# Gated linear attention and a feed-forward layer on one core: the decays of the first two chunk pairs written for both token parities on TensorE, one carried state added by matrix products, and a new written-out order

## The chip, the cores and the metric

The kernel runs on one core of one Trainium2 chip. The time is the device time of one launch in microseconds. Before the change its median over three runs is 182.09 us (181.44 to 182.46).

## The reference

There are two stages. The first is a gated linear recurrence over 768 tokens, for 4 batches of 8 heads with 48 elements each; the second is a feed-forward layer on the 3072 rows of 384 elements that come out of it.

```python
f = 1.0 / (1.0 + np.exp(-f_logit))                 # q, k, v, f_logit: (4, 8, 768, 48) float32
for t in range(S):
    state = f[:, :, t, :, None] * state + np.einsum('bhd,bhe->bhde', k[:, :, t], v[:, :, t])
    y[:, :, t] = np.einsum('bhd,bhde->bhe', q[:, :, t], state)
x = y.transpose(0, 2, 1, 3).reshape(3072, 384)
h = x @ w_in                                       # (384, 2048)
out = (h * np.cos(h)) @ w_out                      # (2048, 384)
```

## The kernel before

**Tiling.** The tokens are cut into 12 pairs of chunks. A pair is 256 tokens of one batch, three pairs to a batch, so pairs 0, 1, 2 are batch 0. Partition p holds the tokens 2p and 2p+1 of the pair, which the code calls the parities e = 0 and e = 1; g = 0, 1 are the two chunks of 128 tokens (the two halves of the partitions), u = 0, 1 are heads 0 to 3 and 4 to 7.

**Steps.** `describe` makes a graph of named steps; a step is one or a few instructions on one engine. For pair n:

- `f`, `k`, `q`, `v`: the loads (line 296), 384 KB each; for pairs 0 and 1 (`HALVES`) the loads of f, k and q are cut into two of 192 KB, `.0` and `.1`.
- `ex`, `ln` (ACT): log(1 + exp(-f)). `cum` (PE): its running sum over tokens, a product with a triangular matrix `incl`. `ei`, `eb` (ACT): exponentials of plus and minus that sum, the decays for k and for q; `eb` also holds the decay of a whole chunk.
- `fx`, `qa`, `ka` and, beyond pair 1, `ad`, `fy`: the running sum is kept for pairs of tokens alone, so the first token of each pair is corrected by hand: `ka` multiplies k by the gate that `fx` makes, `qa` multiplies q by 1 + exp(-f).
- `qm`, `km`: q and k times their decays, into the bfloat16 tile `qk`. `tq`, `tk`: the turn of `qk`, by TensorE with `qkt` as the copy out for pairs 0 to 3; for pairs 4 to 11 `tq` is one DMA transpose on SP's queue.
- `vb`, `vt`: v in bfloat16, and four rearranged copies of it.
- `sc` (PE), `am` (DVE): scores and their mask. `y`, `yi` (PE): the part from within the chunk and the part from the carried state. `xe`: the result as the feed-forward input x.
- `ps` (PE): products of k and v for the state. `st` (DVE): adds the carried state, in two halves of the partitions. `sz` (DVE): times the chunk's decay, giving the next state.

For the feed-forward unit m (the 256 tokens of pair m): `h` is the first product, eight steps of six matmuls; `co` (ACT) the cosine, `g` (DVE) the gate, four each; `o` the second product in row blocks 2m and 2m+1, four steps of four matmuls each; `ot` the copy out of PSUM, `out` the store. `w0.i` and `w1.i` load a quarter of w_in and w_out (768 KB) into a slot of `g`, `wc0.i` and `wc1.i` cast it to bfloat16. `zf` are matmuls on zeros; `ZEROS` is their number. `zsz`, `zqk`, `zsp`, `zvt` clear edges of buffers.

**Order.** `ORDER` lists every step with its engine (T PE, S ACT, V DVE, G POOL, Y SP's queue) and its buffer slots. Each engine runs its steps strictly in that order. Nothing reorders them at run time; an engine waits for what the step at its head needs.

```python
zf48:T2 zf49:T2 zf50:T2 zf51:T2 h0.11:T2 h0.10:T yi1:T7,6 st1.11:V sz1.11:V3 y1:T xe1.1:V2
```

Of the kernel before, what the change touches and what calls it, by code (L numbers as in the profile page):

```python
# [37 lines left out]
zf0:T0 zf1:T0 zf2:T0 zf3:T0 zf4:T0 zf5:T0 zf6:T0 zf7:T0 zf8:T0 zf9:T0 zf10:T0 cum0.0:T4 zvt.1:G
fx0.0:S zqk.0:G zsz.2:G k0.1:Y2 ka0.1:G cum0.1:T7 ei0.1:S1 km0.1:G0 eb0.0:S1 ei0.0:S ex1.0:S eb0.1:S
q0.0:Y0 v0:Y0 vb0:S0 ln1.0:S2 qa0.0:V qm0.0:V zsz.3:G zf11:T0 zf12:T0 zf13:T0 zf14:T0 zf15:T0  # L40
zf16:T0 zf17:T0 zf18:T0 zf19:T0 zf20:T0 zf21:T0 zf22:T0 zf23:T0 zf24:T0 cum1.0:T1 k0.0:Y ka0.0:G
km0.0:V zf25:T0 ps0.0:T6,7 f1.1:Y ex1.1:S ps0.1:T q0.1:Y ei1.0:S0 eb1.0:S0 ln1.1:S fx1.1:S qa0.1:V
sz0.01:V2 sz0.00:V st0.11:V f2:Y1 vt0.1:G2 zvt.0:V st0.10:V vt0.3:G qm0.1:G tk0.0:T0 tq0.0:T
qkt0.0:V0 v1:Y2 vt0.0:G ex2:S ln2:S1 k1.0:Y1 fx1.0:S zsp.1:G k1.1:Y zf26:T2 tk0.1:T6 zf27:T2 tq0.1:T
cum1.1:T3 qkt0.1:V1 zsz.1:G zsz.0:G zf28:T2 sc0.0:T4 am0.0:V2 sc0.1:T0 ad2:G0 sz0.10:V0 am0.1:V0
ei1.1:S eb1.1:S vb1:S1 vt1.2:S0 zf29:T2 zf30:T2 zf31:T2 zf32:T2 cum2:T2 ei2:S2 eb2:S2 ka1.0:V
zqk.1:G km1.0:V1 zf33:T6 zf34:T6 zf35:T6 zf36:T6 zf37:T6 zf38:T6 zf39:T6 zf40:T6 tk1.0:T4 ps1.0:T6,1
f3:Y0 ex3:S q1.0:Y1 sz0.11:V qa1.0:V q1.1:Y qa1.1:V qm1.1:V ln3:S0 fx3:S ka1.1:G vt0.2:G km1.1:G
ps1.1:T y0:T3,5 yi0:T xe0.0:S0 vt1.3:S vt1.1:S fy3:S st1.01:V st1.00:V sz1.01:V1 zf41:T0 zf42:T0
zf43:T0 tq1.1:T0 sz1.00:V qm1.0:G tq1.0:T qkt1.0:S2 tk1.1:T qkt1.1:V0 zf44:T2 zf45:T2 zf46:T2  # L50
zf47:T2 sc1.1:T6 xe0.1:V fx2:S ad3:G1 cum3:T0 ei3:S1 sc1.0:T4 am1.1:V1 am1.0:V3 w0.1:Y0 vt1.0:G
wc0.1:G zf48:T2 zf49:T2 zf50:T2 zf51:T2 h0.11:T2 h0.10:T yi1:T7,6 st1.11:V sz1.11:V3 y1:T xe1.1:V2
st1.10:V sz1.10:V eb3:S1 co0.1:S3 xe1.0:S g0.1:V3 fy2:S w0.0:Y1 wc0.0:G h0.01:T4 h0.00:T h1.01:T6
co0.0:S0 g0.0:V h1.00:T co1.0:S1 g1.0:V2 h1.10:T0 h1.11:T co1.1:S2 g1.1:V k3:Y2 ka3:G km3.1:G2
w0.3:Y4 wc0.3:G h0.31:T2 h0.30:T w0.2:Y0 wc0.2:G h1.21:T4 h1.20:T h0.20:T6 co0.3:S3 g0.3:V co1.2:S0
# [662 lines left out]
```

## Time and profile before

| what | us |
|---|---|
| median of three runs | 182.09 |
| span of the profiled execution | 179.3 |
| PE busy (share of the span) | 171.0 (95%) |
| DVE, ACT, POOL busy | 137.8, 131.3, 109.2 |
| zero matmuls (line 264), busy | 14.8 |
| first product (line 579), busy | 66.7 |
| second product (line 595), busy | 68.4 |

The span runs from the first to the last instruction of the profiled execution. That execution's own time is not listed apart; the three timed runs are 2.1 to 3.2 us longer than this span, so what lies around the span is taken as 182.09 - 179.3 = 2.8 us. A busy PE includes the zero matmuls, and a matmul counts as busy until its modelled end, so the busy share says when PE had something in hand, not that it ran at its peak.

### The profile page before, as it was taken

Reading aid. Unit: us, or ns where it says so; the run is one execution under the profiler, and the core shown is the slowest. Engines: PE = TensorE matmul, PEld = TensorE weight load, DVE = VectorE, ACT = ScalarE, POOL = GpSimd, SP = SyncE. Lnnn points to the kernel's source line nnn. Section 1 sums busy time; section 2 is a strip of 40 time slices with the busy share of each in tenths; the row PEclk is TensorE's granted clock in tenths of the full one; section 3 lists DMA queues with packets and bytes.
Section 4 is the critical chain, followed back from the end, with each engine's and each line's share of the span. In section 5 each row is a group of like instructions: output and inputs, shape, how many; then the busy total and the mean of one; then the engine's idle time right before and its main releaser. Section 6 shows DMA issues by size and latency. Waiting matters only on the chain.

```text
span 179.3 us, 5727 instructions
## 1 busy us (share of the span) xinstructions
PE 171.0 (95%) x2412; PEld 122.9 (69%) x2414; DVE 137.8 (77%) x206; ACT 131.3 (73%) x185; POOL 109.2 (61%) x139
## 2 busy tenths in 40 slices
PE   7998899999999999999999998999999999999992
PEld 2453568876578866778668885668877766867761
DVE  6379998998894989969899887768689996385330
ACT  3899878886999998988999979858973702364410
POOL 7498699976979998789977295827992000000000
PEclk9999999999999999999999999999999999999999
DMA  6999999999999799999999999959045900004013
GB/s 156 262 261 287 356 324 315 306 274 328 257 257 236 168 190 180 282 277 198 249 203 262 226 254 207 234 131 268 4 106 121 148 0 4 4 0 176 0 50 129
DMA packets 74394, 34.46 MB, mean 192 GB/s; under 512 B 67456, under 2 KB 72832, under 8 KB 74368
## 3 DMA queue, kind: packets, MB, share of 16 engines
q1 hardware_dynamic: 73696, 33.79, 81.4%
q8 instruction: 19, 0.31, 0.8%
q10 hardware_dynamic: 672, 0.30, 0.6%
q14 instruction: 7, 0.06, 0.1%
HBM read 25.17 MB, written 4.72 MB: 167 GB/s over the span
## 4 chain that ended last, share of the span: by engine, by line
PE 69%; DMA 10%; POOL 7%; SPq 5%; DVE 5%; issue 3%; ACT 0%; POOLq 0%; DVEq 0%; ACTq 0%
PE ps L595 29%; PE ps L579 29%; DMA q<-in_q_dram 7%; SPq L296 5%; PE ps L531 4%; DMA qkt<-qk 3%; PE ps L456 3%; POOL qk L404 3%; PE ps L479 1%; POOL sp L363 1%; PE ps L435 1%; DVE qk L404 1%; POOL vt L197 1%; DVE sz L503 1%; PE ps L374 1%
## 5 line engine op out<-in xcount | busy, mean ns | idle before, releaser
L561 DVE TENSOR_TENSOR g<-ps,co 128x1024 bf16<-128x1024 f32 x48 | 57.7, 1221 | 15.3 <-ACT co L584 11.3
L595 PE MATMUL ps<-w_out_bf,g 128*128 128x384 bf16 x384 | 68.4, 326 | 0.0
L579 PE MATMUL ps<-x,w_in_bf 128*128 128x256 bf16 x576 | 66.7, 273 | 0.4 <-issue 0.4
L584 ACT ACTIVATE co<-ps,halfpi 128x1024 bf16<-128x1024 f32 x48 | 52.6, 1115 | 17.7 <-PE ps L579 14.4
L579 PEld LDWEIGHTS <-w_in_bf 128*128 128x128 bf16 x576 | 55.8, 98 | 9.2 <-issue 0.6
L595 PEld LDWEIGHTS <-g 128*128 128x128 bf16 x384 | 36.0, 98 | 21.5
L461 DVE TENSOR_TENSOR am<-ps,pmask 128x1024 bf16<-128x1024 f32 x24 | 28.7, 1215 | 3.6 <-PE ps L456 3.5
L404 POOL TENSOR_TENSOR qk<-q,b 128x384 bf16<-128x384 f32 x22 | 21.9, 1002 | 2.6 <-DVE q L338 1.7
L404 POOL TENSOR_TENSOR qk<-k,bi 128x384 bf16<-128x384 f32 x22 | 21.9, 1007 | 1.6 <-ACT bi L391 1.1
L197 POOL COPY vt<-vb 64x384 bf16<-64x384 bf16 x31 | 15.9, 514 | 1.4
L264 PE MATMUL ps<-zero 128*128 128x512 bf16 x50 | 14.8, 435 | 1.3 <-DVE zero L203 1.2
L503 DVE TENSOR_TENSOR sz<-ps,b 64x192 bf16<-64x192 f32 x40 | 14.2, 354 | 1.9 <-PE ps L479 0.9
L351 POOL TENSOR_TENSOR k<-k,f 128x384 f32<-128x384 f32 (+1 forms) x13 | 11.7, 904 | 6.2 <-DMA k<-in_k_dram 2.9
L197 DVE COPY ot<-ps 128x384 f32<-128x384 f32 (+1 forms) x17 | 8.7, 519 | 8.5 <-PE ps L595 6.0
L341 POOL TENSOR_TENSOR q<-f,q 128x384 f32<-128x384 f32 x10 | 10.0, 999 | 8.1 <-DMA q<-in_q_dram 8.1
L363 POOL TENSOR_TENSOR sp<-ls 128x384 bf16<-128x384 f32 x10 | 10.3, 1029 | 4.4 <-issue 2.2
L497 DVE TENSOR_TENSOR ps<-ps,sz 64x192 f32<-64x192 f32 x32 | 11.7, 366 | 1.4 <-PE ps L479 0.3
L329 ACT ACTIVATE f<-f 128x768 f32<-128x768 f32 (+1 forms) x14 | 10.4, 748 | 2.7 <-DMA f<-in_f_logit_dram 2.5
L197 ACT CAST x<-ps 128x384 bf16<-128x384 f32 x12 | 5.5, 479 | 8.6 <-PE ps L531 8.6
L197 ACT COPY ot<-ps 128x384 f32<-128x384 f32 (+1 forms) x9 | 4.1, 455 | 8.9 <-PE ps L595 8.9
L456 PE MATMUL ps<-qkt 48*64 48x128 bf16 (+1 forms) x320 | 8.6, 219 | 1.9 <-DVE qkt L197 1.0
L264 PEld LDWEIGHTS <-zero 128*128 128x128 bf16 x52 | 5.1, 108 | 6.9 <-issue 2.5
(61 smaller groups left out, 166.2 us busy)
## 6 DMA issues: line engine op xcount, KB each, us to landing
v<-in_v_dram SPq DMA_DIRECT2D x12, 384.0 KB, 6.1
out_dram<-ot SPq DMA_DIRECT2D x22, 192.0 KB, 2.8
f<-in_f_logit_dram SPq DMA_DIRECT2D x10, 384.0 KB, 5.6
k<-in_k_dram SPq DMA_DIRECT2D x10, 384.0 KB, 6.1
q<-in_q_dram SPq DMA_DIRECT2D x10, 384.0 KB, 6.4
g<-in_moe_w_in_dram SPq DMA_DIRECT2D x4, 768.0 KB, 7.5
g<-in_moe_w_out_dram SPq DMA_DIRECT2D x4, 768.0 KB, 7.2
k<-in_k_dram SPq DMA_DIRECT2D x4, 192.0 KB, 5.0
```

The costliest lines, as they stand in the source:

```text
L197: (nc.scalar.copy if e == "ACT" else eng(e).tensor_copy)(out=o, in_=i)
L264: G.step(f"zf{i}", ("PE",), lambda e, dump=dump: nc.tensor.matmul(dump.ap, lhsT=zero[:, 0:128], rhs=zero, start=True, stop=True), writes=[ ...
L351: eng(e).tensor_mul(out=w.ap[:, :, 0, :], in0=w.ap[:, :, 0, :], in1=t.ap[:, :, 0, :])
L363: G.step(f"ad{n}", ("POOL",), lambda e: eng(e).tensor_add(out=sp.ap[:, 0, :, 0:D], in0=soft.ap[:, :, 0, :], in1=soft.ap[:, :, 1, :]), read ...
L404: G.step(f"{nm}{n}.{u}", ("POOL", "DVE") if cut else ("POOL",), lambda e, u=u, j=j, src=src, dec=dec: eng(e).tensor_mul(out=qkp[u][j].ap[: ...
L456: nc.tensor.matmul(o[t0:t1, r, 2 * a + g, :].rearrange("p (e n) -> p e n", e=2), lhsT=wide[s, t0 // 64, :] if turned else wide[s].rearrang ...
L461: G.step(f"am{n}.{u}", ("DVE",), lambda e, u=u, sc=sc: nc.vector.tensor_mul(out=am[u].ap.rearrange("p r b n -> p (r b) n"), in0=sc.ap.rear ...
L503: eng(e).tensor_mul(out=new.ap[s, :, r, :].rearrange("p (u a) n -> p u a n", u=2), in0=view()[s].rearrange("p (u a) n -> p u a n", u=2), i ...
L561: nc.vector.tensor_mul(out=o.rearrange("p b (n e) -> p b n e", e=2), in0=ph.ap.rearrange("p (b e n) -> p b n e", e=2, n=64), in1=co.ap.rea ...
L579: nc.tensor.matmul(ph.ap[:, i * T:(i + 1) * T].rearrange("p (g t) -> p g t", t=C), lhsT=w_in_bf[:, kk, f0:f0 + 128], rhs=xa[:, :, kk, :], ...
L584: G.step(f"co{m}.{j}", ("ACT",), lambda e, ph=ph, co=co: nc.scalar.activation(out=co.ap, in_=ph.ap, func=AF.Sin, bias=halfpi), reads=[ph], ...
L595: nc.tensor.matmul(po.ap[:, 0:DM], lhsT=gT.ap[:, j, i * C:(i + 1) * C], rhs=w_out_bf[:, j, :], start=(po.first and j == 4 * s), stop=(po.f ...
```

## The change

1. **Both parities on TensorE (pairs 0 and 1).** `cum` makes the running sum for each token and no longer for pairs of tokens: per half four products with `incl` or `strict` where there were two. `ei` and `eb` are twice as wide (384 and 388 columns instead of 192 and 196). `fx`, `qa` and `ka` of pairs 0 and 1 (four each) are gone; `qm` and `km` read a decay for each parity.
2. **Carried state by identity products (pair 1).** The four `st1` steps on DVE become `si1.0` and `si1.1` on PE, two products with the identity each, into the same PSUM bank as `ps1`.
3. **Loads.** On SP's queue f3, k3, q3 and v3 stand behind the w_in quarters. The first load is pair 1's f, and f0.0 goes from ACT's queue to SP's.
4. **`ZEROS`** 52 becomes 25, and `ORDER` is another for all 12 pairs and units.

The paths for `VLIE` are new but not taken, since `VLIE` is empty.

```diff
+VLIE = ()
+CARRY_PE = (1,)
-ZEROS = 52
+ZEROS = 25
 ORDER = """
-zvt.2:V zsp.2:V f0.1:Y0 zqk.2:G zsp.0:G f0.0:S ex0.1:S ln0.1:S2 f1.0:Y2 ex0.0:S fx0.1:S ln0.0:S
+f1.0:Y0 zf0:T2 f0.0:Y2 zf1:T1 f0.1:Y zsz.0:G zf2:T4 zsp.2:G v0:Y2 zsz.2:G k1.0:Y0 k0.1:Y1 f1.1:Y
...
+    bbS = slots("bb", [128, 2, 2 * HB + 4], F32)
+    bjS = slots("bj", [128, 2, 2 * HB], F32)
...
-        sp, bt, bi = Val(spS), Val(bS), Val(biS)
+        sp, bt, bi = Val(spS), Val(bbS if cut else bS), Val(bjS if cut else biS)
...
-            te, to = (t, t) if cut else (t.part(lambda a: a[:, :, 0, :]), t.part(lambda a: a[:, :, 1, :]))
+            if cut:
+                continue
+            te, to = t.part(lambda a: a[:, :, 0, :]), t.part(lambda a: a[:, :, 1, :])
...
+        W = HB * len(xe)
 
         def cum(e, o, h0, hn):
             w, un = sp.ap[:, :, h0:h0 + hn, :], hn // 4
-            o = o.ap[:, 0:un * (HB + 4)].rearrange("p (u c) -> p u c", u=un)
-            for x in xe:
-                nc.tensor.matmul(o[:, :, 0:HB], lhsT=incl,
-                                 rhs=w[:, x, :, 0:D].rearrange("p (u h) d -> p u h d", u=un),
-                                 start=(x == 0), stop=False)
+            o = o.ap[:, 0:un * (W + 4)].rearrange("p (u c) -> p u c", u=un)
+            for z in xe:
+                for x in xe:
+                    nc.tensor.matmul(o[:, :, HB * z:HB * z + HB], lhsT=strict if x > z and cut else incl,
+                                     rhs=w[:, x, :, 0:D].rearrange("p (u h) d -> p u h d", u=un),
+                                     start=(z == 0 and x == 0), stop=False)
...
-        for nm, dst, dh, sc, w in (("eb", bt, bth, -1.0, HB + 4), ("ei", bi, bih, 1.0, HB)):
+        for nm, dst, dh, sc, w in (("eb", bt, bth, -1.0, W + 4), ("ei", bi, bih, 1.0, W)):
...
+        both = [Val(ap=ident) for u in us] if n in CARRY_PE else []
         for u in us:
             G.step(f"ps{n}.{u}", ("PE",), lambda e, u=u: outer(e, u), reads=[qkp[u][1], vb],
-                   writes=[ps[g] for g in gs], sums=True)
+                   writes=[ps[g] for g in gs] + both[u:u + 1], sums=True)
...
-            if S0 is not None:
+            if S0 is not None and n in CARRY_PE:
+                def add(e, g=g, S0=S0):
+                    for r in range(2):
+                        nc.tensor.matmul(ps[g].ap[:, 0:HB].rearrange("p (a n) -> p a n", n=D), lhsT=ident,
+                                         rhs=S0.ap[:, :, r, :], start=(ps[g].first and r == 0),
+                                         stop=(ps[g].final and r == 1))
+                G.step(f"si{n}.{g}", ("PE",), add, reads=[S0] + both, writes=[ps[g]], sums=True)
+            elif S0 is not None:
```

Three places of the new order follow, each as it stood and as it stands. Row names give the buffer written, then those read.

On SP's queue before, from f3 on: f3, q1 (two halves), w_in's quarters 1 and 0, k3, w_in's 3 and 2, q3, then w_out's quarters 2 and 0.

```order
L296 DMA f_94<-in_f_logit_dram 128x8x96
L296 DMA q_101<-in_q_dram 128x4x96 x2
L282 DMA g_143<-in_moe_w_in_dram 128x3x512
L282 DMA g_144<-in_moe_w_in_dram 128x3x512
L296 DMA k_99<-in_k_dram 128x8x96
L282 DMA g_147<-in_moe_w_in_dram 128x3x512
L282 DMA g_143<-in_moe_w_in_dram 128x3x512
L296 DMA q_102<-in_q_dram 128x8x96
L282 DMA g_144<-in_moe_w_out_dram 128x4x384
L282 DMA g_147<-in_moe_w_out_dram 128x4x384
```

The two other quarters of w_out came four rows later, behind q2, k2 and v3. On SP's queue after, from k2 on (w_in's quarters 1 and 3 stand just ahead of it): k2, w_in's 0 and 2, q2, w_out's 1, 0 and 3, then f3, v2 and the last quarter, w1.2.

```order
L308 DMA k_100<-in_k_dram 128x8x96
L294 DMA g_149<-in_moe_w_in_dram 128x3x512
L294 DMA g_150<-in_moe_w_in_dram 128x3x512
L308 DMA q_101<-in_q_dram 128x8x96
L294 DMA g_152<-in_moe_w_out_dram 128x4x384
L294 DMA g_151<-in_moe_w_out_dram 128x4x384
L294 DMA g_148<-in_moe_w_out_dram 128x4x384
L308 DMA f_97<-in_f_logit_dram 128x8x96
L308 DMA v_106<-in_v_dram 128x8x96
L294 DMA g_152<-in_moe_w_out_dram 128x4x384
```

Pair 3's loads and the last weights have changed places; w1.2 goes into slot 4 of `g` (g_152), which wc1.1 must have read first.

POOL around the last weight cast, before: the k steps of pair 2 (qk_118), the last cast, then v of pair 2 (vb, vt), and the first steps of pairs 4 and 5.

```order
L404 TENSOR_TENSOR qk_118<-k_97,bi_116 128x8x48 x2
L197 COPY vt_125<-vb_121 64x8x48
L197 CAST w_out_bf<-g_144 128x1536
L197 CAST vb_122<-v_105 128x768
L197 COPY vt_124<-vb_122 64x8x48 x4
L363 TENSOR_TENSOR sp_106<-ls_109 128x8x48
L363 TENSOR_TENSOR sp_108<-ls_110 128x8x48
L341 TENSOR_TENSOR q_102<-f_96,q_102 128x8x48
```

POOL around the last weight cast (the second of these two), after:

```order
L415 TENSOR_TENSOR qk_118<-k_100,bi_116 128x8x48
L195 CAST w_out_bf<-g_148 128x1536
L372 TENSOR_TENSOR sp_109<-ls_110 128x8x48
L195 CAST w_out_bf<-g_152 128x1536
L195 COPY vt_130<-vb_121 64x8x48 x2
L359 TENSOR_TENSOR k_99<-k_99,f_97 128x8x48
L372 TENSOR_TENSOR sp_109<-ls_110 128x8x48
L415 TENSOR_TENSOR qk_120<-k_99,bi_115 128x8x48
L349 TENSOR_TENSOR q_101<-f_97,q_101 128x8x48
L415 TENSOR_TENSOR qk_120<-k_99,bi_115 128x8x48
L349 TENSOR_TENSOR q_102<-f_95,q_102 128x8x48
```

All of pair 3's work on POOL but its `ad` (the sp row between the casts) now follows the last weight cast, and pairs 4 and 5 follow that.

DVE before, from the second state of pair 0 (sz_135) to the first x: a mask of pair 0 (am_131), k and q of pair 1 with their corrections, `st` and `sz` of pair 1's first chunk (sz_136), and the copy qkt.

```order
L503 TENSOR_TENSOR sz_135<-ps_161,b_112 64x4x48
L461 TENSOR_TENSOR am_131<-ps_158,pmask 128x1024
L351 TENSOR_TENSOR k_98<-k_98,f_96 128x4x48
L404 TENSOR_TENSOR qk_118<-k_98,bi_114 128x8x48
L503 TENSOR_TENSOR sz_135<-ps_161,b_112 64x4x48
L338 SCALAR_TENSOR_TENSOR q_101<-f_96,q_101 128x4x48 x2
L404 TENSOR_TENSOR qk_118<-q_101,b_111 128x8x48
L497 TENSOR_TENSOR ps_161<-ps_161,sz_135 64x192 x2
L503 TENSOR_TENSOR sz_136<-ps_161,b_111 64x4x48 x2
L197 COPY qkt_126<-ps_158 128x1024
L197 CAST x_139<-ps_160 128x384
```

DVE after, the same stretch:

```order
L240 MEMSET qk_118 128x32x8
L537 TENSOR_TENSOR ps_166<-ps_166,sz_140 64x192
L543 TENSOR_TENSOR sz_142<-ps_166,bb_124 64x4x48
L415 TENSOR_TENSOR qk_119<-q_102,bb_125 128x8x48
L493 TENSOR_TENSOR am_136<-ps_165,pmask 128x1024
L195 COPY qkt_135<-ps_164 128x1024
L493 TENSOR_TENSOR am_137<-ps_166,pmask 128x1024
L493 TENSOR_TENSOR am_139<-ps_164,pmask 128x1024
L543 TENSOR_TENSOR sz_140<-ps_165,bb_125 64x4x48 x2
L493 TENSOR_TENSOR am_138<-ps_164,pmask 128x1024
L543 TENSOR_TENSOR sz_143<-ps_163,bb_125 64x4x48 x2
L195 CAST x_145<-ps_163 128x384
```

The corrections of q and k (L338, L351) and pair 1's additions are gone from it; three masks now stand ahead of pair 1's first state (sz_140 from ps_165), and a clearing of qk_118 has moved here from POOL.

More of the change, by code (lines that the diff above doesn't have):

```diff
@@ L38 @@
[L38 to L55, printed above, removed]
```

223 lines of the change are left out of this document (138 added, 85 removed).

## The prediction

> **What bounds the kernel now.** I read the page first, then the chain of waits, then stretches. The page's lines give the span and the busy engines.
>
> ```profile
> span 179.3 us, 5727 instructions
> PE 171.0 (95%) x2412; PEld 122.9 (69%) x2414; DVE 137.8 (77%) x206; ACT 131.3 (73%) x185; POOL 109.2 (61%) x139
> ```
>
> The chain (start, duration, what) shows three parts.
>
> ```profile
> 15.37 0.34 DVE sz L503
> ...
> 25.08 1.31 PE ps L579 x12
> ...
> 43.85 0.65 PE ps L595 x4
> ...
> 168.21 7.81 PE ps L595 x48
> ...
> 176.05 0.33 ACT ot L197
> ...
> 176.40 0.36 DVE ot L197
> ```
>
> Until 25.08 DVE and the loads lead to the first feed-forward product; from there to 176.02 PE is the chain but for a detour that costs it little; 3.28 us of copying and storing close it. The stretches (length, then busy PE, PEld, DVE, ACT, POOL, then clock, DMA share, GB/s) say how full PE is.
>
> ```profile
> 25.08:44.50 19.42, 19.42 (x264) 15.45 (x262) 17.28 (x22) 15.72 (x17) 16.31 (x16) 1.00 1.05 309
> 72.10:176.02 103.92, 102.89 (x1432) 76.05 (x1432) 78.18 (x105) 70.08 (x93) 48.97 (x58) 1.00 0.69 149
> 5.00:15.00 10.00, 8.86 (x110) 5.26 (x110) 6.18 (x12) 8.85 (x23) 7.49 (x13) 1.00 1.27 262
> 19.00:23.00 4.00, 3.43 (x95) 2.11 (x95) 3.78 (x9) 3.37 (x7) 3.63 (x4) 1.00 1.11 342
> ```
>
> PE has no idle time from 25.08 to 44.50 and 1.03 us after 72.10. So the end can move only by an earlier first product, by new waits after it, or by the tail. PE's real work after the first product is nearly the same: by steps, the new order puts cum3 (about 0.3 us) and si1.1 (0.2) behind it and yi1 (0.4) ahead, +0.1 us. The fillers on zeros (14.8 us busy) all stand ahead of it and cost only what the wait there leaves.
>
> **Loads.** Consumers that waited give landings: the first half load of f, q0.1 (the tenth half) and w1.3.
>
> ```profile
> 4.04 0.52 ACT L329 ACTIVATE f<-f 128x384 f32<-128x384 f32 x1 [1.50 <-DMA f<-in_f_logit_dram]
> 10.56 0.38 DVE L338 SCALAR_TENSOR_TENSOR q<-f,q 128x192 f32<-128x192 f32 x1 [0.20 <-DMA q<-in_q_dram]
> 44.65 1.46 POOL L197 CAST w_out_bf<-g 128x1536 bf16<-128x1536 f32 x1 [1.30 <-DMA g<-in_moe_w_out_dram]
> ```
>
> At 262 GB/s a half load (197 KB) takes 0.75 us, at 342 GB/s a weight quarter (786 KB) 2.3. From 4.0 on that puts the tenth half at 10.75 (10.56 measured) and w1.3, behind 28 more halves and 8 quarters, at 43.4 (44.65). The new queue then lands k0.0 at 11.5, k1.1 at 16.0, q1.1 at 16.8, w1.0 at 33.6 and w1.2, behind 25 halves and 8 quarters, at 41.2; by the 1.2 us that the check missed, 42.4. I take 41.8.
>
> **Parts and their prices** (line, engine, form, count, then busy us and mean ns):
>
> ```profile
> L347 ACT ACTIVATE f<-sp 128x192 f32<-128x192 bf16 x4 | 1.4, 354 | 0.1
> L338 DVE SCALAR_TENSOR_TENSOR q<-f,q 128x192 f32<-128x192 f32 x4 | 1.4, 363 | 2.6 <-DMA q<-in_q_dram 2.6
> L351 POOL TENSOR_TENSOR k<-k,f 128x192 f32<-128x192 f32 x3 | 1.8, 591 | 2.2 <-DMA k<-in_k_dram 2.1
> L391 ACT ACTIVATE bi<-ps 128x192 f32<-128x192 f32 x4 | 1.3, 328 | 0.9 <-PE ps L380 0.9
> L395 ACT ACTIVATE bi<-ps 128x384 f32<-128x384 f32 x10 | 4.7, 489 | 1.5 <-PE ps L380 1.5
> L497 DVE TENSOR_TENSOR ps<-ps,sz 64x192 f32<-64x192 f32 x32 | 11.7, 366 | 1.4 <-PE ps L479 0.3
> L503 DVE TENSOR_TENSOR sz<-ps,b 64x192 bf16<-64x192 f32 x40 | 14.2, 354 | 1.9 <-PE ps L479 0.9
> L461 DVE TENSOR_TENSOR am<-ps,pmask 128x1024 bf16<-128x1024 f32 x24 | 28.7, 1215 | 3.6 <-PE ps L456 3.5
> L404 DVE TENSOR_TENSOR qk<-q,b 128x384 bf16<-128x384 f32 x2 | 2.5, 1234 | 0.7 <-ACT b L391 0.6
> L404 DVE TENSOR_TENSOR qk<-k,bi 128x384 bf16<-128x384 f32 x2 | 1.1, 558 | 0.7 <-POOL k L351 0.7
> L197 DVE COPY qkt<-ps 128x1024 bf16<-128x1024 bf16 x6 | 4.0, 677 | 0.1
> L561 DVE TENSOR_TENSOR g<-ps,co 128x1024 bf16<-128x1024 f32 x48 | 57.7, 1221 | 15.3 <-ACT co L584 11.3
> L584 ACT ACTIVATE co<-ps,halfpi 128x1024 bf16<-128x1024 f32 x48 | 52.6, 1115 | 17.7 <-PE ps L579 14.4
> L584 ACT ACT_TABLE_LOAD x5 | 6.4, 1283 | 0.1
> ```
>
> Both parities: ACT loses four fx (1.4 us) and pays eight wider exponentials, 8 x 0.16 = 1.3, nothing on balance. DVE loses four qa (1.4) and one ka, POOL three ka (1.8); the eight extra cum products are a few tenths of PE in a stretch full of fillers. Identity products: four st of 0.366 leave DVE. All this counts only as far as it lies on the way to the first product, which I now follow.
>
> ACT's two exponentials of pair 1 begin at 4.0, those of pair 0 when f0.1 has landed (5.5); four steps of 0.52, then ei1.0, ei0.1, eb1.0, eb0.1, ex1.1, eb0.0 and ei0.0 at 0.5 end at 11.1. km0.0 on POOL starts with k0.0 at 11.5 and ends at 12.5; PE, with fillers and cum1.1 queued ahead, has ps0.0 at 13.4. From here DVE is the chain: four sz, two st and a clearing, 2.5 us, to 16.0; qm1.0; am0.1, qkt1.0, am0.0, am1.0 and two sz, 5.0; some 0.3 of starts. yi1 (0.4) and a filler (0.2) follow on PE. qm1.0 costs 0.56 or 1.23, and these rows tell why:
>
> ```profile
> 7.74 0.99 POOL L404 TENSOR_TENSOR qk<-k,bi 128x384 bf16<-128x384 f32 x1 [1.13 <-ACT bi L391]
> 7.85 1.30 DVE L404 TENSOR_TENSOR qk<-q,b 128x384 bf16<-128x384 f32 x1 [0.57 <-ACT b L391]
> 9.81 0.56 DVE L404 TENSOR_TENSOR qk<-k,bi 128x384 bf16<-128x384 f32 x1 [0.66 <-POOL k L351]
> ```
>
> Beside a running POOL product the same form ends 0.42 after POOL's end; alone it takes 0.56. km1.1 starts on POOL with k1.1 at 16.0, just when DVE comes to qm1.0. So the first product starts at 22.4 (0.56) to 23.1 (1.23); I take 22.8, 2.3 us before the 25.08 of now. The Trainium skill's page "SBUF — State Buffer", section "SBUF: two separate sides", states it as an exclusive lock: a DVE operation with two SBUF inputs and a GpSimd operation that reads SBUF exclude each other for a whole instruction. The rows agree; by that rule with POOL first the product starts at 23.1, without any lock at 22.4, which reaches the end only in the first rival below.
>
> **What takes the head start back.** The first co begins some 3.0 us after the first product (an h step 0.65, y1 0.6 behind am1.1, si1.1 and a filler 0.4, an h step 0.65, and what shows of the 1.28 us reload of ACT's table, 0.7). Seven co at 1.115, fy2 (0.5) and wc1.0 (1.46 like the cast above), with 0.4 of waits for g, bring ACT to 22.8 + 13.2 = 36.0, when o3.0 may start; the h steps, held to DVE's 1.22 a gate, are done before that. Nine o steps and pair 2's small products, 6.8 us, then lead PE to o1.2 at 42.8. o1.2 needs w1.2: landed 41.8, cast by POOL 1.46, 43.3. w1.2 must also wait for its slot; wc1.1 frees it near 33, and 7 us for the transfer fit in. So o1.2 starts at 43.2 and the early start has become a wait of some tenths at the last weight.
>
> How does that stand to now? At 44.50 in the chain (the end of the row at 43.85) the old order has 130.7 us of PE steps left by my count at the chain's prices (0.65 an h or o step; 1.3 us of idle come on top); at o1.2 the new one has 131.25. 44.50 + 130.7 = 175.2 against 43.2 + 131.25 = 174.45: 0.75 us gained here.
>
> **POOL and the transposes.** Behind wc1.2 POOL has all of pair 3 and then 4 and 5: 20 products, 8 vt, 2 vb until km5.0.
>
> ```profile
> 57.72 2.92 POOL L404 TENSOR_TENSOR qk<-k,bi 128x384 bf16<-128x384 f32 x3
> L197 POOL COPY vt<-vb 64x384 bf16<-64x384 bf16 x31 | 15.9, 514 | 1.4
> L197 POOL CAST vb<-v 128x768 bf16<-128x768 f32 x7 | 5.8, 822 | 0.1
> DMA to landing us min/median/max: 3.1/4.1/6.7
> ```
>
> 20 x 0.97 + 8 x 0.51 + 2 x 0.82 = 25.1 us, then tq5.0 by DMA (last row: the 16 transposes), 4.1: 29.2 after the cast. PE has 28.8 us from o1.2 to sc5.0. So sc5.0 waits 0.4, between nothing (3.1) and 3.0 (6.7). Now POOL is ahead at that point: it ended the last cast at 46.1 with most of pairs 2 and 3 done. Pairs 6 to 11 have 3 us and more in hand by the same count. The whole cost of the deferral is this wait; the cover is those 28.8 us of PE work.
>
> **Tail.** The last step is now o21.1, whose 192 KB leave in one piece.
>
> ```profile
> out_dram<-ot SPq DMA_DIRECT2D x6, 192.0 KB, 2.1
> out_dram<-ot SPq DMA_DIRECT2D x3, 96.0 KB, 1.6
> ```
>
> The store takes 0.5 more, but one copy of 0.47 replaces two in a row (0.33 + 0.36): +0.25.
>
> **Sum**, against the span of 179.3: -0.75 + 0.4 + 0.25 = -0.1, or 179.2; with the 2.8 that lie around it 182.0. The waits at w1.2 and sc5.0 are the two large unknowns. Half of the landing check's miss may not recur, so I take 181.8: no change that can be told, 0.5% (0.9 us) being about what a measurement of this kernel tells.
>
> **Rivals.** *The head start stays.* If w1.2 is cast by 41.5 and ACT is not late with wc1.0, nothing holds PE: -2.3 + 0.1 + 0.25 = -1.95, 180.1. For it: the loads ahead of w1.2 are 0.6 MB fewer than ahead of w1.3 now. Against it: ACT's count above alone gives 36.0 at o3.0.
> *Pair 5 is late: slower.* The cast ends at 44.0, km5.0 at 69.1, and a transpose of 6.0 lands at 75.1. By the same count of steps left PE now stands there at 72.9, so +2.2, with the tail 184.5. It decides from a cast plus transpose 1.5 us later than I took. For it: SP's queue has tq5.1, a store and q7 ahead of tq5.0.
> *A cold TensorE: slower.*
>
> ```profile
> 1.19 4.88 PE L264 MATMUL ps<-zero 128*128 128x512 bf16 x11 [1.19 <-DVE zero L203]
> 7.09 3.21 PE L264 MATMUL ps<-zero 128*128 128x512 bf16 x14
> ```
>
> Eleven fillers go at 0.43 us each, from 7.09 fourteen at 0.23: PE took 5.9 us of work to reach full rate, though the profile's clock reads 1.00 throughout. With 25 fillers, and none from 2.5 to 5, PE might be at half rate at the first products: 5.9 us of them at half rate lose 2.9, of which the 1.4 us of waits that follow absorb part; +1.5, 183.6. Against it: my count leaves no gap over 1.5 us between 5 and 22.8. The Trainium skill's page "TensorE: Matmul & The Clock Gate", Part 1, has the half rate return only after an idle window of about 3.4 us; by that rule the clock stays up.
>
> **How the numbers follow.** No change 0.39; head start (or most of it) kept 0.37; pair 5 late 0.17, cold PE 0.04, no head start because DVE's chain is longer than counted (first product at 25, o1.2 at 45.0, a loss of 1.05 for the gain of 0.75, no wait at sc5.0: 183.4) 0.03. So faster 0.37, same 0.39, slower 0.24. The range for 8 in 10 runs from the kept head start with 0.5 more at the weights, 179.6, to the late pair 5, 184.3; that of the likeliest case alone is 181.2 to 182.7.
>
> **What would show it.** The first L579 row near 22.8; no fx, qa, ka of pairs 0 and 1; PE waiting at a second product for a w_out cast, near 36 and 43; PE waiting at L471 for a transpose near 72; the last store of 192 KB. A first product later than 23.5, w1.2 landing before 40 or after 43, or idle PE beyond 75 would make the prediction wrong.

## The result, and the profile after

The new kernel takes 187.93 us (median of four runs, 186.65 to 189.02) where the old one takes 182.21 on the same chip: ratio 1.0316, 95% interval 1.0239 to 1.0393. It is slower by 5.7 us; 181.8 was predicted, and the range ended at 184.3. The profiled execution took 189.02 us and its span is 6.8 us longer than the old one's. The page's first lines and TensorE's row of the slices:

```profile
span 186.1 us, 5682 instructions
PE 169.2 (91%) x2399; PEld 122.0 (66%) x2399; DVE 130.1 (70%) x193; ACT 134.0 (72%) x187; POOL 109.4 (59%) x138
PE   3888999899999969799997997998999999999992
```

TensorE is busy for 91% of the span where it was 95%, and the slices behind its first feed-forward product that are not full lie, but for one near 35, in the middle, between 65 and 131 us. Stretches of the same profile (length, busy PE, PEld, DVE, ACT, POOL, clock, DMA share, GB/s), cut at the first feed-forward product, at o1.2, behind the last wait and at the end of TensorE's work:

```profile
22.59:43.05 20.46, 19.67 (x217) 14.89 (x214) 13.70 (x15) 18.88 (x24) 15.78 (x16) 1.00 1.10 322
43.05:131.00 87.95, 81.12 (x1272) 59.85 (x1268) 66.19 (x94) 75.90 (x107) 70.45 (x86) 1.00 0.95 205
131.00:182.46 51.46, 51.46 (x661) 37.15 (x658) 35.79 (x48) 23.45 (x30) 9.21 (x13) 1.00 0.29 66
182.46:186.10 3.64, 0.00 (x1) 0.00 (x0) 0.00 (x0) 0.48 (x1) 0.00 (x0) 1.00 0.39 133
```

The first product starts at 22.59, 2.49 us earlier than before. Between 43.05 and 131.00 TensorE is idle for 6.83 us; behind 131.00 never. The old kernel had 1.2 us of idle time in all behind its first product, which started at 25.08. The chain of waits (start, duration, what) names two of the places:

```profile
68.50 0.53 SPq L660
...
69.08 5.68 DMA q<-in_q_dram
...
74.92 0.04 POOL q L349
...
80.11 1.24 DVE g L615
...
81.39 5.41 PE ps L633 x48
...
109.25 5.37 DMA out_dram<-ot
...
114.72 0.57 DVE ot L195
...
115.33 1.48 PE ps L633 x12
```

Up to the product at 81.39 the end hangs on the load q7 on SP's queue, at 115.33 on a store whose buffer a copy had to wait for. Five of TensorE's waits (us in total, times, longest):

```profile
PE ps L471 <- DMA qkt<-qk: 1.6, 1, 1.6
PE ps L471 <- DVE g L615: 1.4, 1, 1.4
PE ps L633 <- DVE ot L195: 1.2, 1, 1.2
PE ps L633 <- ACT x L195: 1.0, 1, 1.0
PE ps L571 <- ACT bi L406: 0.8, 1, 0.8
```

L471 is the scores: the first row is sc5.0, the second sc4.1. The second names DVE's g by mistake: the g that ended at 69.50 is g3.3, which stands behind sc4.1 in the order and reads another bank. The g that had to leave sc4.1's bank, g3.2, ended at 68.11; tq4.1 landed at 69.46, and sc4.1 started at 69.50. So both waits are for transposes. The last row lies inside y6, which waits twice, first for ACT's copy ot9 and then for ACT's exponentials. On ACT the copy stands ahead of those exponentials, and it waited itself for the buffer that the store out7 left at 97.65:

```profile
97.75 0.48 ACT L195 COPY ot<-ps 128x384 f32<-128x384 f32 x1 [1.75 <-DMA out_dram<-ot]
```

For a finer account I take from the trace, for every step of TensorE, how much later it starts than it would straight behind the step ahead, and count 0.2 us and more ("waits" from here on; one is some 0.16 longer than its idle time, since the step ahead then no longer overlaps). New: o3.0 0.92, y3 0.24, sc4.1 1.57, sc5.0 1.80, h4.31 0.50, y6 0.58 and 0.94 inside the step, h6.10 1.35, h8.30 1.13, together 9.0. Old: sc5.0 0.34, sc8.0 0.80 and 0.54 inside h4.31, together 1.7. So the span's 6.8 us are: the start -2.49, waits +7.35, steps that changed sides +0.35 (cum3, si1.1 and a zero product, 0.7, now stand behind the first product, and yi1, 0.35, ahead of it), the tail +0.36 (3.64 against 3.28), and 1.25 that is left. Some 0.3 of that is starts late by less than 0.2 each; the rest lies in the spacing of the steps, which depends on what follows what (see e13 below).

### The profile page after: what moved, and what is told of

It reads as the page before. It is cut to its first block, busy times and chain, and to the rows that moved or that the text cites. A ratio compares the mean times of both kernels' runs of the same rounds, so it can differ in the third digit from the quotient of the medians.

```text
span 186.1 us, 5682 instructions
## 1 busy us (share of the span) xinstructions
PE 169.2 (91%) x2399; PEld 122.0 (66%) x2399; DVE 130.1 (70%) x193; ACT 134.0 (72%) x187; POOL 109.4 (59%) x138
## 4 chain that ended last, share of the span: by engine, by line
PE 53%; DMA 13%; POOL 11%; SPq 8%; DVE 6%; issue 4%; ACT 3%; ACTq 0%; POOLq 0%; DVEq 0%
PE ps L633 22%; PE ps L649 22%; DMA q<-in_q_dram 5%; DMA out_dram<-ot 5%; POOL qk L415 5%; SPq L439 4%; DMA k<-in_k_dram 3%; PE ps L571 3%; POOL vt L195 2%; SPq L308 2%; DVE g L615 2%; PE ps L471 2%; ACT co L638 2%; POOL k L359 2%; SPq L660 1%
## 5 line engine op out<-in xcount | busy, mean ns | idle before, releaser
L649 PE MATMUL ps<-w_out_bf,g 128*128 128x384 bf16 x384 | 68.4, 326 | 0.8 <-DVE g L615 0.8
L415 POOL TENSOR_TENSOR qk<-q,b 128x384 bf16<-128x384 f32 x20 | 19.8, 997 | 0.6
L415 POOL TENSOR_TENSOR qk<-k,bi 128x384 bf16<-128x384 f32 x20 | 19.9, 997 | 0.2
L195 POOL COPY vt<-vb 64x384 bf16<-64x384 bf16 x35 | 17.6, 507 | 2.3 <-ACT vb L195 0.7
L195 ACT COPY ot<-ps 128x384 f32<-128x384 f32 (+1 forms) x13 | 5.9, 454 | 15.3 <-PE ps L649 8.9
L543 DVE TENSOR_TENSOR sz<-ps,b 64x192 bf16<-64x192 f32 x32 | 11.3, 353 | 1.8 <-PE ps L571 0.8
L195 DVE COPY ot<-ps 128x384 f32<-128x384 f32 (+1 forms) x13 | 6.6, 520 | 8.1 <-PE ps L649 5.0
L471 PE MATMUL ps<-qkt 48*64 48x128 bf16 (+1 forms) x320 | 9.2, 220 | 3.0 <-DMA qkt<-qk 1.6
L537 DVE TENSOR_TENSOR ps<-ps,sz 64x192 f32<-64x192 f32 x28 | 10.3, 366 | 1.8 <-PE ps L511 0.9
L471 PEld LDWEIGHTS <-qkt 48*64 48x64 bf16 (+1 forms) x320 | 5.9, 104 | 7.3 <-DMA qkt<-qk 3.5
L359 POOL TENSOR_TENSOR k<-k,f 128x384 f32<-128x384 f32 x10 | 9.9, 998 | 0.2
L276 PE MATMUL ps<-zero 128*128 128x512 bf16 x25 | 8.7, 439 | 1.4 <-DVE zero L201 1.2
```

The costliest lines, as they stand in the source:

```text
L195: (nc.scalar.copy if e == "ACT" else eng(e).tensor_copy)(out=o, in_=i)
L359: eng(e).tensor_mul(out=w.ap[:, :, 0, :], in0=w.ap[:, :, 0, :], in1=t.ap[:, :, 0, :])
L415: G.step(f"{nm}{n}.{u}", ("POOL", "DVE") if cut else ("POOL",), lambda e, u=u, j=j, src=src, dec=dec: eng(e).tensor_mul(out=qkp[u][j].ap[: ...
L471: nc.tensor.matmul(o[t0:t1, r, 2 * a + g, :].rearrange("p (e n) -> p e n", e=2), lhsT=wide[s, t0 // 64, :] if turned else wide[s].rearrang ...
L537: nc.vector.tensor_add(out=view()[s], in0=view()[s], in1=S0.ap[s, :, r, :])
L543: eng(e).tensor_mul(out=new.ap[s, :, r, :].rearrange("p (u a) n -> p u a n", u=2), in0=view()[s].rearrange("p (u a) n -> p u a n", u=2), i ...
```

## Experiments

All ratios are to the old kernel on the same chip, with 95% intervals. Four theories: **D** (order and fill of SP's queue make pairs 4 to 9 late; called Q in the first runs, and its weaker form is the order alone), **P** (POOL is late since pair 3 was put off), **T** (ACT's table reloads), **C** (TensorE's late full rate).

**One row, one store, less POOL work, and the new start alone.**

e1, SP's rows:

```diff
-tq5.1 out5 q7 tq5.0
+tq5.1 tq5.0 q7 out5
```

> The new kernel with two rows of SP's queue moved: the store out5 and the load q7 stand behind the transpose tq5.0 and no longer ahead of it. In the new kernel sc5.0 waited 1.8 us for that transpose (issued 69.6, landed 75.7, behind q7's 384 KB). Theory Q (what stands ahead in SP's queue makes the transposes late): tq5.0 lands 2.5 to 3 us earlier, the wait at sc5.0 goes, and 1 to 1.8 us of span come back (ratio about 1.024). Theory P (POOL is late from pair 4 on because pair 3 was put off, and whatever is late there is paid by PE sooner or later): the wait at sc5.0 goes, q7 lands 2 to 3 us later, POOL's work on pair 7 with it, and PE pays the same at a later place: ratio 1.03 as before.

e2, SP's rows (`ot6` is the copy on ACT):

```diff
-ot6 ... out7 ... out9 ... out8 tq8.1 tq8.0 k9 out1 out6 q9
+ot6 out6 ... out7 ... out9 ... out8 tq8.1 tq8.0 k9 out1 q9
```

> The new kernel with one row of SP's queue moved: the store out6 stands right behind its copy ot6 and no longer 17 us later behind tq8.1, tq8.0, k9 and out1. In the new kernel h6.10 waited 1.35 us for a copy whose buffer that store had to leave (landed 114.6). Theory Q: that wait goes, and 1.0 to 1.35 us of span come back (ratio about 1.025). Theory P: pair 8 and 9 are late by as much anyway, the wait moves to the next step that needs POOL: ratio 1.03.

e3:

```diff
+            if n in (3, 4):
+                continue
             G.step(f"qa{n}{u}", ("POOL",), ...
             G.step(f"ka{n}{u}", ("POOL",), ...
```

> The new kernel without the corrections qa and ka of pairs 3 and 4 (four POOL products of 1.0 us; those pairs' q and k stay uncorrected). POOL has no pause from 49 to 69 us, so tq4.1 and tq5.0 can be issued up to 4 us earlier. Theory P: the waits at sc4.1 (1.57) and sc5.0 (1.80) go, and 2.5 to 3.5 us of span come back (ratio about 1.015). Theory Q: only the part that POOL sets goes, the queue's part of the wait at sc5.0 stays, and 1.6 us or less come back (ratio 1.023 or more). A third theory, that ACT's reloads of its table make the later waits (h4.31, y6, h8.30, together 2.2 us), expects these three unchanged.

e4, the old order in the new code (the last line names the words taken out of it):

```diff
-CARRY_PE = (1,)
-ZEROS = 25
+CARRY_PE = ()
+ZEROS = 52
-fx0.0 fx0.1 fx1.0 fx1.1 qa0.0 qa0.1 qa1.0 qa1.1 ka0.0 ka0.1 ka1.0 ka1.1
```

> The kernel before, in its old order, with the decays of both parities of pairs 0 and 1 on TensorE alone: the steps fx, qa and ka of these pairs are gone, the carried state stays on DVE, loads and the 52 zero products stay. If the new start as such were what costs, this would be slower than before by 1% or more. The theories P and Q, in which the loss sits behind 50 us, expect a first feed-forward product 0 to 1.5 us earlier than 25.1 and a ratio between 0.99 and 1.00.

Measured: e1 1.0293 (1.0218 to 1.0369), e2 1.0408 (1.0305 to 1.051), e3 1.0397 (1.0311 to 1.0483), e4 0.9969 (0.9924 to 1.0014). The intervals of e1, e2 and e3 overlap the new kernel's (1.0239 to 1.0393), and e1's holds the numbers of both theories; these three are read from their traces.

In e1 the wait at sc5.0 is gone, the one at sc4.1 is shorter (0.83), and the feed-forward step h4.31 starts 2.8 us earlier than in the new kernel; at the end 1.5 of it is left, since sc6.1 now waits 1.09 and y6 0.4 longer. So nearly half of what was won is lost at the next waits, as P says. In e2 the wait at h6.10 is gone, and TensorE's end is 0.25 earlier; but in that run 1.7 us went to a stretch at half rate (last section), so its end does not tell whether the wait came back. And e3 took 4 us of work from POOL, yet sc5.0 waited 1.83 as before and sc4.1 still 1.07. A row of e3's POOL shows what replaced the work:

```profile
51.38 0.82 POOL L192 CAST vb<-v 128x768 bf16<-128x768 f32 x1 [2.27 <-DMA v<-in_v_dram]
```

POOL waited for v3, which landed at 51.3 here and at 51.8 in the new kernel. P in its plain form falls. e4 says that the new decays as such cost nothing: the first product came at 24.1 (24.9 in the same count before), the end 0.5 earlier.

**What the late part hangs on.**

e5:

```diff
-out=co.ap, in_=ph.ap, func=AF.Sin, bias=halfpi), reads=[ph], writes=[co], table="S")
+out=co.ap, in_=ph.ap, func=AF.Identity, bias=halfpi), reads=[ph], writes=[co])
```

> The new kernel with ACT's cosine replaced by a plain copy plus a constant of the same shape (L638), so that ACT never reloads its table (13 reloads of 1.28 us in the new kernel, 9 in the old one); the cosine is left out. Theory T (the reloads make PE wait: two of them sit behind the wait of the cosine they serve, at 77.6 and 127.2): the waits at h4.31, y6 and h8.30, 2.2 us together, go, and 2 to 3 us of span come back (ratio 1.015 to 1.02). Theory D (the stream of loads, stores and transposes is full until some 85 us and sets when pairs 4 to 9 can be used) and theory P (POOL sets it): less than 1 us comes back, the waits at sc4.1 and sc5.0 stay.

e6 (`h0, h1` are the heads that a load brings):

```diff
-load(f"{kind}{n}", whole, src, b, c, 0, H)
+load(f"{kind}{n}", *((hs[0], src, b, c, 0, 4) if kind in "qk" and n > 2 and f"{kind}{n}" != "q5" else (whole, src, b, c, 0, H)))
```

> The new kernel with the loads of k and q of pairs 3 to 11 cut to heads 0 to 3 (q5 stays whole); heads 4 to 7 of these pairs compute on old data. 17 loads of 1.5 us become 17 of 0.75: 12.7 us less in the stream of transfers, no instruction of another engine changes. Theory D: the waits at sc4.1 and sc5.0 and most of the later ones go, and 4 to 6 us of span come back (ratio 1.00 to 1.01). Theory P: POOL, which had no pause from 49 to 69 us, stays as late, and 1.5 us or less come back (ratio 1.024 or more). Theory T: nothing at h4.31 and h8.30.

e7: as e3, with `if n > 2`.

> The new kernel without the corrections qa and ka of pairs 3 to 11: 18 POOL products of 1.0 us gone (q and k of these pairs stay uncorrected). Theory P: POOL is ahead from pair 4 on and 4 to 6 us of span come back (ratio 1.00 to 1.01). Theory D: POOL waits for the loads instead, as it did without four of these products, and 1.5 us or less come back (ratio 1.024 or more).

e8, SP's rows from q4 to tq9.1 (further rows behind that are moved too, and loads, transposes, nine output buffers and one of `qk` take another of their slots):

```diff
-q4 k4 v3 v4 k5 out0 q5 f6 f7 tq4.0 out3 k6 v5 k7 q6 tq4.1 tq5.1 out5 q7 tq5.0 v6 q8 v9 v7 f8 tq7.1
-out4 f11 tq6.0 k8 f9 tq6.1 v8 tq7.0 out7 k10 out9 v10 k11 f10 out8 tq8.1 tq8.0 k9 out1 out6 q9 tq9.1
+q4 v4 v3 k4 k5 out0 q5 f6 f7 tq4.0 out3 q7 v5 k6 tq4.1 k7 tq5.1 tq5.0 q6 f11 v6 v7 f8 v9 tq7.1
+out1 out4 tq6.0 f9 tq6.1 out6 tq7.0 q8 k8 out7 v8 k9 f10 out9 tq8.1 v11 out8 q9 v10 k10 k11 tq8.0 tq9.1
```

> The new kernel with SP's rows behind w1.2 in another order, and nothing else moved: transposes ahead of the loads around them (tq5.1 and tq5.0 ahead of q6), the loads of q, for which POOL waits first, ahead of those of k (q7 ahead of k6, q8 and q9 earlier), stores later where no buffer waits for them (out5, out10, out15) and earlier where one does (out6, out1). The bytes are the same. Theory D in its weaker form (the order of the rows, not the number of bytes, makes pairs 5 to 9 late): 2.5 to 4 us of span come back (ratio 1.01 to 1.018). If the number of bytes, POOL or ACT sets it: less than 1.5 us (ratio 1.024 or more).

Measured: e5 1.0259 (1.0185 to 1.0333), e6 1.0099 (1.0055 to 1.0144), e7 1.0211 (1.0136 to 1.0287), e8 1.0064 (1.0015 to 1.0113).

e8 moves the same bytes in another order and brings back 2.5% of the 3.2%, the most of the four and more than was expected of it. (Its q8 went later, where the expectation says earlier; POOL reads it only at 96.) e7 lies between the numbers of P and D, and its interval overlaps the new kernel's. SP's queue in the new kernel, then in e8, around pair 5 (start, time until SP was free again, what):

```profile
59.01 0.39 SPq L308 DMA_DIRECT2D k<-in_k_dram  x1
59.45 0.65 SPq L308 DMA_DIRECT2D v<-in_v_dram  x1
60.15 1.91 SPq L308 DMA_DIRECT2D k<-in_k_dram  x1
62.11 1.23 SPq L308 DMA_DIRECT2D q<-in_q_dram  x1
63.51 4.90 SPq L439 DMA_TRANSPOSE qkt<-qk  x2
68.50 0.53 SPq L660 DMA_DIRECT2D out_dram<-ot  x1
69.08 0.43 SPq L308 DMA_DIRECT2D q<-in_q_dram  x1
69.60 2.37 SPq L439 DMA_TRANSPOSE qkt<-qk  x1
```

```profile
59.89 0.45 SPq L305 DMA_DIRECT2D q<-in_q_dram  x1
60.38 0.64 SPq L305 DMA_DIRECT2D v<-in_v_dram  x1
61.06 1.39 SPq L305 DMA_DIRECT2D k<-in_k_dram  x1
64.00 1.30 SPq L436 DMA_TRANSPOSE qkt<-qk  x1
65.35 0.58 SPq L305 DMA_DIRECT2D k<-in_k_dram  x1
67.58 3.41 SPq L436 DMA_TRANSPOSE qkt<-qk  x2
```

In the new kernel k6, v5, k7 and q6 (four loads of 384 KB) stand ahead of tq4.1 and tq5.1, and out5 and q7 ahead of tq5.0; q7, which POOL reads before q6, is asked for last. They landed in the order of the queue: k6 63.65, v5 65.11, k7 67.35, q6 68.58, tq4.1 69.46. In e8 q7 comes first and tq5.0 has neither q6 nor a store ahead of it. POOL's waits show the other side, the new kernel first, then e8's longest three:

```profile
POOL q L349 <- DMA q<-in_q_dram: 8.9, 4, 4.7
```

```profile
POOL sp L369 <- ACT ls L342: 12.4, 5, 4.7
POOL vb L192 <- DMA v<-in_v_dram: 4.6, 1, 4.6
POOL qk L412 <- DMA k<-in_k_dram: 2.2, 2, 1.1
```

q is gone from POOL's longest waits, POOL now waits longest for ACT's `ls`, and TensorE's waits at sc4.1 and sc5.0 (3.37) shrink to 0.21, those at y6 and h6.10 (2.87) to nothing; h4.31 and h8.30 keep theirs. A part of this is chance: e8's profiled run had a late first product, and TensorE came to sc4.1 at 69.9 where it came at 68.1 in the new kernel. But e9 below has e8's rows and the early start. There TensorE comes to sc4.1 at 68.4 and to sc5.0 at 73.2, tq4.1 has landed at 68.1 and tq5.0 at 72.7 (69.5 and 75.7 in the new kernel), and neither product waits.

Fewer bytes in the new kernel's order of rows (e6, 12.7 us of loads less) also cleared sc4.1 and sc5.0, in a run that started 2.0 us late, and brought back 2.2%. So D holds: a better order of the same bytes takes away most of the loss, and so do fewer bytes in the same order. Which of e8's moves counted is not told apart. P got 1 of its expected 2 to 3% in e7, with 18 us of POOL work gone and sc4.1 and sc5.0 still waiting 2.96.

e5 took the waits at h4.31 and h8.30 away, as T expected, and the reason can be read in the new kernel's ACT:

```profile
77.62 1.28 ACT L638 ACT_TABLE_LOAD   x1 [3.34 <-issue]
78.91 1.11 ACT L638 ACTIVATE co<-ps,halfpi 128x1024 bf16<-128x1024 f32 x1
```

The reload had 3.3 us to spare and started only when h4.00 was done (77.55): it stands behind the wait of the cosine that it serves. But the ratio fell by 0.6% only, less than the intervals can tell; sc5.0, y6 and h6.10 still waited.

**The start again.**

e9 (e8 with) and e10 (the new kernel with):

```diff
-ZEROS = 25
+ZEROS = 32
-zf2:T4 zsp.2:G ... zf5:T5 ei1.0:S0 ... zf7:T4 eb1.0:S1
+zf2:T4 zf25:T4 zf26:T4 zf27:T4 zf28:T4 zsp.2:G ... zf5:T5 zf29:T2 ei1.0:S0 ... zf7:T4 zf30:T4 zf31:T4 eb1.0:S1
```

> SP's rows reordered as in the run before it (e8), and seven more products on zeros in the gaps that TensorE has before the first feed-forward product (four after zf2, one after zf5, two after zf7; ZEROS 32). In e8's profiled run the zeros still took 0.43 us each until 13.4 us and the first feed-forward product stood at 24.4; in the profiled run of the new kernel they took 0.22 from 9.0 on and it stood at 22.4. Theory C (with few zeros TensorE's full rate comes at 9 or at 13.5, by chance): the zeros take 0.22 from 8 to 9 us on, the first product stands at 22.2 to 22.6, and with the queue's order mended the end follows by 1 to 2 us (ratio 0.997 to 1.002). Theory D (after 50 us the stream of transfers sets the end, whatever the start): the first product comes earlier, the end does not: ratio 1.006 as e8.

> The new kernel with the same seven more products on zeros and nothing else changed. Theory D: the first product comes at 22.2 to 22.6 in every run and the end stays, ratio 1.025 to 1.032. If a late full rate of TensorE were a large part of the loss, 1.5 to 2 us would come back (ratio 1.02).

e11 (e9 with, in the loop that writes the steps out):

```diff
+            if s.table == "S" and table != "S":
+                nc.scalar.preload_act_table_set("trig_and_small")
```

> As e9, and each reload of ACT's table for the cosine is issued ahead of the wait of the cosine (in the new kernel two of seven stood behind it, at 77.6 and 127.2). Theory T: the waits at h4.31 (0.5) and h8.30 (1.13), which e8 kept, go, and 1 to 1.6 us of span come back against e9. Without it: no difference from e9.

e12:

```diff
-CARRY_PE = (1,)
+CARRY_PE = ()
-si1.0:T ... si1.1:T
+st1.01:V st1.00:V ... st1.10:V st1.11:V
```

> The new kernel with the identity products undone: the carried state of pair 1 is added by DVE in four steps st1, as in the old kernel, at the places where si1.0 and si1.1 stood. Two steps of 0.37 lie on DVE's way to yi1 and to the first feed-forward product, which comes 0.5 to 0.8 us later. If the head start counted, the end would be later by as much (ratio 1.035); theory D expects the later waits to shrink by it and the end to stay (ratio 1.028 to 1.032).

Measured: e9 1.0055 (1.0034 to 1.0076), e11 1.0037 (0.9998 to 1.0076), e12 1.0363 (1.0326 to 1.04); e10 186.71 us against 182.02 (four runs from 184.66 to 188.74, spread too far for a verdict). Of e11 only the times are read: it is 0.2% below e9, within the intervals, so T's 1 to 1.6 us did not show.

e9's first product stood at 22.4 where e8's stood at 24.4, and its TensorE ended 0.85 earlier; the median did not move by more than the interval. In this pair of profiled runs a start 2 us earlier is worth less than half of itself, even with the rows mended. e10 does not settle its question. e12's profiled run had both the slow zeros (below) and DVE's steps, a first product at 24.4, and a TensorE end only 0.9 later than the new kernel's: its waits at sc4.1 and sc5.0 were 2.43 where they had been 3.37. As in e9, part of a shift at the start is gone at pair 5. Its ratio is the one expected if the head start counted (1.035), above D's 1.028 to 1.032, but the new kernel's interval reaches as far; the price of the identity products alone stays open.

**Why the mended kernel stays 0.4 to 0.6% behind.** e13 is e11, e14 is e4 with e11's edit, both with the rows of every engine behind the weights in another order, found by a search over a model of the queues fed with measured durations; about a third of the rows move.

> e11 with the rows of every engine behind w1.3 put in another order by a search over a model of the queues (about a third of the rows move); pair 3 stays behind the weights, the decays, identity products, the seven more zeros and the early table reloads stay. If badly placed rows of the other engines are what is left of the loss: 1 to 2 us less than e11, ratio 0.992 to 0.998, faster than before. If the deferral itself costs: no better than e11, ratio 1.002 to 1.006.

> The old order with the decays of both parities on TensorE alone (e4: carried state on DVE, 52 zeros, pair 3 ahead of the weights), its rows put in another order by the same search, and the early table reloads. If the deferral costs: 0.5 to 1 us less than e4, ratio 0.990 to 0.995, and clearly less than e13. If it does not: within 0.3% of e13.

Measured: 1.0211 (1.0176 to 1.0247) and 1.0196 (1.0157 to 1.0234). Neither version gained. e14 lies within 0.3% of e13, which was to mean that the deferral costs nothing, but both carry a new loss that hides it. The stretch from the first product to TensorE's end, e9 first, then e13:

```profile
22.42:177.82 155.40, 152.37 (x2140) 111.93 (x2139) 115.62 (x156) 118.43 (x159) 95.97 (x113) 1.00 0.78 180
23.47:181.04 157.57, 155.70 (x2140) 111.76 (x2139) 115.84 (x156) 118.70 (x159) 94.24 (x112) 1.00 0.77 176
```

The same 2140 matmuls keep TensorE busy 3.3 us longer with less idle time. The steps' starts show where: in both runs an o step is followed by the next o step after 0.65 us and by a scores step after 0.74, and a scores step by another after 0.25 and by an o step after 0.33 to 0.35. So a change between the feed-forward layer's steps and the small products costs 0.09 to 0.1 us each way, while a change from h to o costs nothing (0.655, as from h to h). e13 has 98 such changes in this stretch and e9 62; 36 more at 0.09 are the 3.3 us. (e14 has 88, e4 58.) The search knew the waits and not this price.

For e9 the trace shows what is left against the old kernel, a span 2.2 us longer in spite of a first product 2.5 us earlier: waits of 0.92 at o3.0, 0.50 at h4.31, 0.62 at o11.1, 1.13 at h8.30 and two of 0.2 to 0.5 against 1.7 in all, some 1.35 of steps that changed sides or have other neighbours (62 changes against 58 are 0.4 of it), a tail 0.4 longer and small late starts. How much of that the deferral as such causes stays open.

e15 (e4 with) and e16 (e15 with the identity products):

```diff
-tq5.1 f9 tq5.0 ... v9 v8 k9 q9 ... tq8.1 f11 q10 f10 tq8.0
+tq5.1 tq5.0 f9 ... q9 v9 v8 k9 ... tq8.1 tq8.0 f11 q10 f10
```

> The old order with the decays of both parities on TensorE (e4) and three rows of SP's queue moved: f9 behind tq5.0, q9 ahead of v9, tq8.0 ahead of f11. In e4's profile sc5.0 waited 0.7 us for tq5.0, sc8.0 0.35 for tq8.0, and POOL 3 us for q9. Theory D: these waits go, 0.5 to 1 us less than e4: ratio 0.990 to 0.995 and faster than before. If the stream's bytes alone decide: as e4, 0.997.

> e15 with the carried state of pair 1 added by identity products (si1.0 behind ps1.1, si1.1 behind yi1) and no longer by DVE. DVE loses four steps of 0.37, two of them ahead of the first feed-forward product; TensorE gains 0.33. If DVE leads there: the first product 0.3 to 0.7 us earlier and a ratio 0.1 to 0.4% below e15. If the loads or the zeros in front of the first product lead: no difference, or 0.1% slower.

In both tq8.0 now stands ahead of its product qm8.0 and turns old data, so part of pair 8 is left out of the computation. Measured: 0.9933 (0.9905 to 0.9961) and 0.9985 (0.9951 to 1.0019). tq5.0 landed 1.6 us earlier than in e4, and yet sc5.0 waited 1.37 where it had waited 0.71: the profile names ACT's `bi`, not the transpose. f9, put behind, is read on ACT ahead of those exponentials and landed at 71.1. e16, which was to lie 0.1 to 0.4% below e15 or at most 0.1% above, lies 0.5% above it, with intervals that just touch: the identity products gained nothing in the old order.

e17 (e4 with):

```diff
-v9 v8 k9 q9 ... tq8.1 f11 q10 f10 tq8.0
+q9 v9 v8 k9 ... tq8.1 f11 tq8.0 q10 f10
```

> e4 with q9 ahead of v9, and q10 and f10 behind tq8.0 (f9 and tq5.0 as in e4). POOL waited 3 us for q9 in e4 and qm8.0 stands behind that wait; sc8.0 waited 0.35 us for tq8.0. Theory D: q9 lands at 96 where it landed at 102, tq8.0 at 106 to 108 where it landed at 111, the wait at sc8.0 goes and the next ones with it: ratio 0.991 to 0.996. If only waits of TensorE that the profile shows count: 0.35 us, ratio 0.995. If the stream's bytes alone decide: 0.997 as e4.

Measured: 180.67 us against 182.09, ratio 0.9947 (0.9916 to 0.9977): half a per cent below the old kernel, with an interval clear of 1. q9 landed at 96.3 (102.0 in e4), tq8.0 at 108.3 (111.1), and the wait at sc8.0 went. It lies within D's numbers and at the edge of the others', and its interval overlaps e4's; how much of the gain is the two moves is not told apart.

## Why the prediction was wrong

- **The start: right.** 22.8 predicted, 22.59 measured; qm1.0 took 0.56. The rows of the new kernel, then of e8, with DVE's product and POOL's beside it:

```profile
16.36 0.56 DVE L415 TENSOR_TENSOR qk<-q,bb 128x384 bf16<-128x384 f32 x1
16.61 1.17 POOL L415 TENSOR_TENSOR qk<-k,bj 128x384 bf16<-128x384 f32 x1 [0.97 <-ACT vt L195]
```

```profile
17.46 1.00 POOL L412 TENSOR_TENSOR qk<-q,bb 128x384 bf16<-128x384 f32 x1
17.83 1.04 DVE L412 TENSOR_TENSOR qk<-q,bb 128x384 bf16<-128x384 f32 x1
```

  Who starts first keeps its time, and the other ends late: POOL's 1.17 here is 0.17 over its usual 1.00, DVE's 1.04 in e8 ends 0.41 behind POOL's end. That is the exclusive lock of the Trainium skill, page "SBUF — State Buffer", section "SBUF: two separate sides", and the trace agrees with it to within 0.15 us (POOL's product ends 0.86 behind DVE's end where alone it takes 1.00).
- **Loads and the way to o1.2: right.** w1.0 33.2 (33.6), w1.2 40.4 (41.8), o3.0 at 35.94 (36.0), o1.2 at 43.05 to 43.2 (43.2), though by TensorE's own work and not by the cast, which ended at 42.4. By the prediction's own count of the steps left the gain of 0.75 stood there.
- **POOL and the transposes: the step that failed.** "25.1 us to km5.0" was near (26.4, from 42.4 to 68.8). The transpose behind it was taken at its median, 4.1, as if nothing stood ahead of it in SP's queue; it took 6.9 from the product's end to its landing at 75.67, with out5 and q7 ahead of it. In e1, with neither ahead, it landed at 72.5. And sc4.1, which waited 1.57 for tq4.1 behind four loads, was not in the count at all. Predicted wait 0.4, measured 3.4. The rival "pair 5 is late" named this mechanism and SP's queue as its reason, with 0.17 and a price of 2.2; the 187.93 measured lies beyond its 184.5 too.
- **"Pairs 6 to 11 have 3 us and more in hand by the same count": wrong.** They waited 4.5 us (h4.31, y6, h6.10, h8.30). The count had POOL's work and TensorE's, and none of SP's rows. y6 and h6.10, 2.9 of it, hang on the stores out7 and out6 and are gone in e8; h4.31 and h8.30, 1.6, stayed in e8 and went in e5, so they are ACT's late reloads, which the prediction put at nothing behind the first cosine. e8 shows that SP's rows, not POOL's work, were the larger part of the whole loss: by the difference of the two ratios 2.5 of the 3.2%.
- **Tail: right** (+0.25, measured +0.36). **TensorE's work behind the start** was taken at +0.1; the steps that changed sides are +0.35, and some 1.0 more lies in the spacing of the steps, which was no term of the sum (four more changes of the kind priced in e13, 62 against 58, are 0.4 of it; the rest is not told apart).
- **The bounds on "what would show it"**: idle TensorE beyond 75 was named as what would make the prediction wrong, and that is what happened.

## What to carry to other kernels

Where one queue carries loads, stores and transposes, write down for each waiting step what stands ahead of it in that queue, and give each row the time behind those rows, not its median; rows should stand in the order in which their readers run, transposes first, stores where no buffer waits for them (e8 did all of this at once, so the runs don't rank these rules). But look at who else reads a row that is moved back: each is the head of another engine's order. A head start is worth only what the next shared stream can deliver earlier, and an order found by a model is to be measured: what it leaves out (here the price of a change between large and small products) is where it will put the cost.
